# One held PSUM bank instead of two in a fast matrix product, GpSimd's sums cut in halves and rationed, and the last batch on attention's banks

## The chip, the cores and the metric

The kernel runs on one core of one Trainium2 chip. The metric is the device time of one execution in microseconds (us), median of several runs. All inputs lie in HBM when it starts, and all outputs must lie there when it ends. The engines of the core are TensorE (PE; its weight loads are listed apart as PEld), VectorE (DVE), ScalarE (ACT), GpSimd (POOL) and SyncE (SP, which here only issues transfers). Each runs its own list of instructions in order and waits for the others by semaphores.

## The reference

Two blocks one after the other, all in float32: attention that keeps the 32 largest scores of each row, then a Fourier mixing block with a two-layer MLP.

```python
# q, k, v: (8, 8, 576, 64): batch, heads, sequence, head dimension
scores = (1 / sqrt(64)) * matmul(q, k^T)
kth    = the 32nd largest score of each row
scores = where(scores >= kth, scores, -1e9)
attn   = softmax(scores)
a      = matmul(attn, v)
x      = a, heads side by side                      # (8, 576, 512)
mixed  = real(fft(fft(x, axis=1), axis=2))
u      = x + mixed
un     = (u - mean(u)) / sqrt(var(u) + 1e-6)        # over the 512 channels
out    = u + maximum(un @ w_ch1, 0) @ w_ch2         # w_ch1: 512x2048, w_ch2: 2048x512
```

## The kernel before

The program is written out by a Python loop over 288 steps of attention (32 pairs of heads, 9 tiles of 128 rows each) and a few more. In one step VectorE finds the 32 largest scores of one tile (four `max` of eight values and three `match_replace`), GpSimd turns two of those maxima into a shift and a bound (`nt`), ScalarE and GpSimd mask the scores, ScalarE takes the exponential (`expo`), and TensorE computes scores three tiles ahead, transposes the weights of two tiles back (`tpP`) and multiplies them with v (`o`). The work of the Fourier block and of the MLP of the batch before is put between these as "units" in a queue, so many in each step that it comes out even.

```python
    def bounds(i):                                   # end of step i, GpSimd
        Nt[i] = small.tile([P, 2], F32, name=f"nt_{i}", tag="nt", bufs=6)
        nc.gpsimd.tensor_tensor(out=Nt[i], in0=M8.pop(i)[:, 0:TOPK:TOPK - 1], in1=cc, op=ALU.mult)

    def mask(i):                                     # step i + 1
        w = Wk[i]
        nc.scalar.activation(out=w, in_=Ssb[i], func=AF.Relu, scale=-FAR, bias=Nt[i][:, 1:2])
        nc.gpsimd.tensor_tensor(out=w, in0=Ssb.pop(i), in1=w, op=ALU.subtract)
```

PSUM has eight banks. Attention holds five: two for scores (`ps_s`, tag "sp"), two for transposes (`ps_t`, tag "tp"), one for its output (`ps_o`). Everything else takes the three banks of `ps_m` in turn. A caller may hold one; the others then share what is left.

```python
    held, turn = set(), [0]

    def bank(shape, name, hold=False):
        while turn[0] in held:
            turn[0] = (turn[0] + 1) % 3
        n = turn[0]
        turn[0] = (n + 1) % 3
        t = ps_m.tile(shape, F32, name=name, tag=f"m{n}", bufs=1)
        if not hold:
            return t
        held.add(n)
        return t, lambda: held.discard(n)
```

Users of `bank` are the transform over tokens (`yp`, four a batch, each emptied by three ScalarE instructions), the transform over channels (`mp`, five a batch, emptied by ScalarE, or by VectorE in the first and last batch), the transposes before the MLP (`tpu`, five), the hidden layer (`hp`, 32), the second layer of the rest rows (`cp`) and the fast product below. The folds in front of the token transform (`sd`, `zw`, `fg`) run on GpSimd in batches 1 to 6; in the last batch half of them run on VectorE.

The second layer, hidden @ w_ch2, is done for batches 1 to 7 with seven products of half-size blocks in place of eight (`fast`, once for each of two chunks of 256 rows, 8 matmuls a product, two units a product). It needs four sums over the hidden layer (`mix`, GpSimd, 128x1024 each) and sums of the weights, which come in streamed. Two banks are held: X from `p1` to `p3`, Y from `p4` until VectorE has added the last two products.

```python
            def mix(dst, a, c, op=ALU.subtract):
                v = h()
                nc.gpsimd.tensor_tensor(out=v[dst], in0=v[a], in1=v[c], op=op)

            def summed(t, cols, src, n):                       # ScalarE empties, GpSimd adds
                ...                                            # (last batch: one VectorE instruction)
                nc.scalar.mul(out=room(n), in_=src, mul=rs[:, t:t + 1])
                nc.gpsimd.tensor_tensor(out=xt, in0=xt, in1=room(n), op=ALU.add)

            def p1(part):
                if part == 0:
                    got["X"], got["free X"] = bank([P, 2, DH], f"cx_{b}_{ch}", True)
                    mix("21", "21", "22", ALU.add)
                product(got["X"][:, 0, :], "11", b11, part, True)
                if part:
                    nc.scalar.copy(out=room(0), in_=got["X"][:, 0, :])
                    mix("11", "21", "11")
            def p4(part):    # Y, first half: "22" x T4; then summed(), mix("22", "22", "11")
            def p2(part):    # X, first half, on top of p1: "12" x B21; then summed(), mix("12", "12", "11")
            def p5(part):    # X, second half: "21" x T1; then summed()
            def p6(part):    # Y, first half: "11" x T2
            def p7(part):    # Y, second half: "22" x T3; then VectorE adds both halves to room(0), ...
            def p3(part):    # X, second half: "12" x B22; then summed(), X is freed, store
            # units in the order p1, p4, p2, p5, p6, p7, p3
```

At the end of a step come the lists of planned work; `pool0` (folds) runs before `bounds`, so a `mix` or a fold in front of it delays `nt` of that step. The sums of the weights are made once, every second step, four GpSimd instructions at a time:

```python
    for kc in range(NK):
        at(PER_BATCH + 14 + 2 * kc, "pool", lambda kc=kc: parts_of_w2(kc))
    ...
        run(i, "pool0")
        bounds(i)
```

Attention's output of a pair goes to token rows in `to_tokens` (`tpx`), which from the second batch on takes the bank of `ps_o`, one or more steps after `attend` has filled it (`o`); VectorE empties it at the end of the step. If the rows of x are not free yet, it waits in `pending`, and may then fall in a step in which `attend` fills the same bank again.

Of the kernel before, what the change touches and what calls it, by code (L numbers as in the profile page):

```python
# [9 lines left out]
F32 = mybir.dt.float32  # L10
# [54 lines left out]
def kernel(  # L65
# [544 lines left out]
    def dft_tokens(b, par, g2):  # L610
# [6 lines left out]
        y = y_of[b]  # L617
        yp = bank([P, 2, KQ], f"yp_{b}_{par}_{g2}")

# [38 lines left out]
    def dft_channels(b, t, quick=False):  # L658

        rows, y = ROWS[t], y_of[b]  # L660
        mp = bank([P, 2, DM // 2], f"mp_{b}_{t}")
        for par in range(2):
# [61 lines left out]
    def channels_first(b, t):  # L724

        rows = ROWS[t]
        ch, col = CHUNK_OF[t]
        if (b, ch) not in unT_of:
            unT_of[b, ch] = batp.tile(
                [P, NDT, CW[0]], F32, name=f"unT_{b}_{ch}", tag="fold_s" if ch == 0 else "y"  # L730
            )
        tp = bank([P, NDT, P], f"tpu_{b}_{t}")
        for dt in range(NDT):
            nc.tensor.transpose(
                tp[:, dt, 0:rows], x_of[b][0:rows, t, P * dt:P * (dt + 1)], ident[0:rows, 0:rows]
            )
        nc.scalar.copy(out=unT_of[b, ch][:, :, col:col + rows], in_=tp[:, :, 0:rows])  # L737
        return 0.6


# [14 lines left out]
    for _ in range(B - 1):  # L755
        for ch in range(2):
            stream += [(o, kc) for o in (T4, B21, T1, T2, T3) for kc in range(NK)]
            if ch == 0:
                stream += [(o, kc) for kc in range(NK) for o in (T1, B21)]
# [32 lines left out]

    def parts_of_w2(kc):

        t = batp.tile([P, 4, DH], F32, name=f"w2_t_{kc}", tag="fold_d")
        lo, hi = w2[:, kc, :], w2[:, NK + kc, :]
        for out_, in0, in1 in (
            (T1, lo[:, DH:], lo[:, 0:DH]), (T2, hi[:, DH:], t[:, T1]),
            (T3, hi[:, DH:], lo[:, DH:]), (T4, hi[:, 0:DH], t[:, T2]),
        ):  # L800
            nc.gpsimd.tensor_tensor(out=t[:, out_], in0=in0, in1=in1, op=ALU.subtract)
        at(now[0] + 1, "load2", lambda: nc.sync.dma_start(out=scr[:, 0:4, kc, :], in_=t))

    def mlp_units(b):
# [110 lines left out]
        def fast(ch):  # L917

            ta, tb = CHUNKS[ch][0], CHUNKS[ch][1]
            rs, got = rs_of[b], {}  # L920
            lo, hi = slice(0, DH), slice(DH, DM)
# [7 lines left out]

            def room(n):  # L930
                if ch == 0:
                    if not cts:
                        cts.append(batp.tile([P, 3, DM], F32, name=f"ct_{b}", tag="fold_s"))
                    return cts[0].rearrange("p t c -> p (t c)")[:, DH * n:DH * (n + 1)]
                o = NIT * CW[1] + DH * n
                return hTs[1].rearrange("p i c -> p (i c)")[:, o:o + DH]

            def product(dst, a, of, part, start=False):
                for kc in range(NK // 2 * part, NK // 2 * (part + 1)):
                    rhs, done = of(kc)  # L940
                    nc.tensor.matmul(  # L941
                        dst, lhsT=h()[a][:, kc, :], rhs=rhs, start=start and kc == 0,
                        stop=kc == NK - 1, skip_group_check=True,
                    )
                    done()

            def summed(t, cols, src, n):

                xt = x[:, t, cols]
                if last:  # L950
                    nc.vector.scalar_tensor_tensor(
                        out=xt, in0=src, scalar=rs[:, t:t + 1], in1=xt, op0=ALU.mult, op1=ALU.add
                    )
                    return
                nc.scalar.mul(out=room(n), in_=src, mul=rs[:, t:t + 1])
                nc.gpsimd.tensor_tensor(out=xt, in0=xt, in1=room(n), op=ALU.add)

            def mix(dst, a, c, op=ALU.subtract):
                v = h()
                nc.gpsimd.tensor_tensor(out=v[dst], in0=v[a], in1=v[c], op=op)  # L960

            def streamed(o):
                return lambda kc: take(o, kc)

            def store(t, steps):
                def go():
# [8 lines left out]
                else:  # L975
                    at(now[0] + steps, "load2", go)

            def p1(part):
                if part == 0:
                    got["X"], got["free X"] = bank([P, 2, DH], f"cx_{b}_{ch}", True)  # L980
                    mix("21", "21", "22", ALU.add)
                product(got["X"][:, 0, :], "11", b11, part, True)
                if part:
                    nc.scalar.copy(out=room(0), in_=got["X"][:, 0, :])
                    mix("11", "21", "11")

            def p4(part):
                if part == 0:
                    got["Y"], got["free Y"] = bank([P, 2, DH], f"cy_{b}_{ch}", True)
                product(got["Y"][:, 0, :], "22", streamed(T4), part, True)  # L990
                if part:
                    summed(tb, lo, got["Y"][:, 0, :], 2)
                    mix("22", "22", "11")

            def p2(part):
                product(got["X"][:, 0, :], "12", streamed(B21), part)
                if part:
                    summed(ta, lo, got["X"][:, 0, :], 3)
                    mix("12", "12", "11")

            def p5(part):
                product(got["X"][:, 1, :], "21", streamed(T1), part)
                if part:
                    summed(tb, hi, got["X"][:, 1, :], 2)

            def p6(part):

                product(got["Y"][:, 0, :], "11", streamed(T2), part, True)

            def p7(part):  # L1010
                product(got["Y"][:, 1, :], "22", streamed(T3), part)
                if not part:
                    return
                u2, u3, Y = room(0), room(1), got["Y"]

                def both():
                    nc.vector.tensor_tensor(out=u2, in0=Y[:, 0, :], in1=u2, op=ALU.add)
                    nc.vector.tensor_tensor(out=u3, in0=Y[:, 1, :], in1=u2, op=ALU.add)
                    got["free Y"]()

                def spread():
                    xa, xb = x[:, ta, hi], x[:, tb, :].rearrange("p (e c) -> p e c", e=2)
                    u3s = u3.rearrange("p (e c) -> p e c", e=1).to_broadcast([P, 2, DH])
                    if last:
                        for xt, u, t in ((xb[:, 0], u3, tb), (xb[:, 1], u3, tb), (xa, u2, ta)):
                            nc.vector.scalar_tensor_tensor(
                                out=xt, in0=u, scalar=rs[:, t:t + 1], in1=xt,
                                op0=ALU.mult, op1=ALU.add,
                            )
                    else:  # L1030
                        nc.scalar.mul(out=u3, in_=u3, mul=rs[:, tb:tb + 1])
                        nc.scalar.mul(out=u2, in_=u2, mul=rs[:, ta:ta + 1])
                        nc.gpsimd.tensor_tensor(out=xb, in0=xb, in1=u3s, op=ALU.add)
                        nc.gpsimd.tensor_tensor(out=xa, in0=xa, in1=u2, op=ALU.add)
                    store(tb, 1)

                if last:
                    both()
                    spread()
                else:  # L1040
                    def later():
                        both()
                        at(now[0] + 1, "act", spread)
                    late_next.append(later)

            def p3(part):
                product(got["X"][:, 1, :], "12", b22, part)
                if part:
                    summed(ta, hi, got["X"][:, 1, :], 3)
                    got["free X"]()  # L1050
                    store(ta, 3)

            def tails(half, part):
# [20 lines left out]
                (1.75, lambda f=f, part=part: f(part), "back")  # L1074
                for f in (p1, p4, p2, p5, p6, p7, p3) for part in range(2)
            ]
# [131 lines left out]
    for kc in range(NK):  # L1208
        at(PER_BATCH + 14 + 2 * kc, "pool", lambda kc=kc: parts_of_w2(kc))
    at(PER_BATCH + 14, "load2", lambda: nc.sync.dma_start(out=scr[:, B21], in_=w2[:, NK:, 0:DH]))  # L1210
# [102 lines left out]
    i, carry = 0, 0.0  # L1313
    while i < N + 4 or plan or queue:
        now[0] = i
# [21 lines left out]
        tok = []  # L1337
        if pending and pending[0][0] <= i:
            _, pp, pc = pending[0]
# [66 lines left out]
        for n in range(max(len(first), len(second))):  # L1406
            for ops in (first, second):
                if n < len(ops):
                    ops[n]()

        run(i, "pool0")
        bounds(i)
        if i < PER_BATCH:
# [46 lines left out]
```

## Time and profile before

| | before |
|---|---|
| device time, median of 3 runs | 1966.39 us (1964.42 to 1966.81) |
| profiled execution, span | 1964.0 us |
| PE busy | 1806.4 us (92%) |
| DVE busy | 1591.4 us (81%) |
| ACT busy | 1225.0 us (62%) |
| POOL busy | 961.6 us (49%) |

Attention and the MLPs of batches 0 to 6 fill the time up to about 1775 us. What is left is the transform and the MLP of the last batch. In a line of the costliest groups, the first word is the kernel's line, then the engine, the operation, what is written and read, shapes and count; after the bar come the busy time in us, the mean of one in ns, the idle time of the engine before them, and what ended it. A busy PE need not be one at its peak: matmuls are pipelined and their ends modelled. PEclk is the granted TensorE clock, 1.00 being full speed.

### The profile page before, as it was taken

The page shows a single profiled execution, that of the slowest core. Times are in us where ns is not written, and L with a number is a line of the kernel's source. Part 1 is how long each engine was busy: PE and PEld are TensorE (multiplying, and loading weights), DVE is VectorE, ACT ScalarE, POOL GpSimd, SP SyncE. Part 2 cuts the span into 40 slices and gives each one's busy share as a digit, 9 for nine tenths or more (in the row PEclk, how much of TensorE's full clock was granted, in tenths as well). Part 3 has the DMA queues.
Part 4 walks back from the last instruction along what each step waited for, and adds up shares of the span by engine and source line. Part 5 has one row for each costly group of instructions (what it writes and reads, how often), then busy time and mean ns, then how long its engine had stood idle before and what let it go on. Part 6 is the DMA issues. An engine that isn't in the chain of part 4 may idle for free.

```text
span 1964.0 us, 30502 instructions
## 1 busy us (share of the span) xinstructions
PE 1806.4 (92%) x9520; PEld 1275.7 (65%) x9520; DVE 1591.4 (81%) x3284; ACT 1225.0 (62%) x3128; POOL 961.6 (49%) x1196
## 2 busy tenths in 40 slices
PE   6666799998999999999999999999999999998899
PEld 3443465565667676776667776666667776676677
DVE  8999989998999979987888969897889878852110
ACT  6878657776767667665766757566666657651111
POOL 4767544636443663446525554436525464434111
PEclk8777899999999999999999999999999999999999
DMA  5323002210224130322204241242304241133151
GB/s 163 111 83 103 19 13 62 75 45 25 62 71 130 40 115 19 107 85 81 73 19 136 60 126 29 68 121 62 88 18 126 76 119 30 51 113 107 44 163 44
DMA packets 235633, 151.37 MB, mean 77 GB/s; under 512 B 135248, under 2 KB 226512, under 8 KB 235472
## 3 DMA queue, kind: packets, MB, share of 16 engines
q1 hardware_dynamic: 234688, 149.22, 26.4%
q8 instruction: 76, 1.25, 0.3%
q14 instruction: 85, 0.70, 0.1%
q10 hardware_dynamic: 784, 0.21, 0.0%
HBM read 134.65 MB, written 14.68 MB: 76 GB/s over the span
## 4 chain that ended last, share of the span: by engine, by line
PE 69%; POOL 15%; ACT 6%; issue 5%; DVE 5%; DMA 0%; SPq 0%; POOLq 0%; DVEq 0%; ACTq 0%
PE hp L820 23%; PE cx L941 7%; PE o L465 7%; PE cy L941 6%; PE sp L363 5%; PE tpP L428 5%; POOL wk L401 4%; PE yp L622 3%; PE cp L1064 3%; PE mp L670 3%; POOL hT L960 2%; PE cp L844 2%; DVE m L384 2%; POOL w L215 2%; POOL w L214 2%
## 5 line engine op out<-in xcount | busy, mean ns | idle before, releaser
L401 POOL TENSOR_TENSOR wk<-S,wk 128x576 f32<-128x576 f32 x288 | 408.2, 1417 | 753.4 <-ACT wk L400 725.3
L384 DVE MAX8 m<-wk 128x8 f32<-128x576 f32 x864 | 624.0, 751 | 5.2
L820 PE MATMUL hp<-unT,w 128*128 128x256 f32 (+1 forms) x2048 | 537.4, 409 | 3.7 <-ACT unT L737 2.1
L820 PEld LDWEIGHTS hp<-unT,w 128*128 128x128 f32 x2048 | 372.7, 190 | 127.9 <-issue 29.0
L386 DVE MATCH_REPLACE8 wk<-m,wk 128x576 f32<-128x576 f32 x576 | 427.9, 743 | 0.0
L400 ACT ACTIVATE wk<-S,nt 128x576 f32<-128x576 f32 x288 | 226.8, 788 | 94.4 <-POOL nt L393 93.4
L407 ACT ACTIVATE wk<-wk,nt 128x576 f32<-128x576 f32 x288 | 224.6, 780 | 75.6 <-POOL wk L401 74.2
L428 PE MATMUL tpP<-ident,wk 128*128 128x128 f32 x1152 | 187.6, 288 | 75.1 <-ACT wk L407 51.2
L428 PEld LDWEIGHTS tpP<-ident,wk 128*128 128x128 f32 x1152 | 143.0, 147 | 141.1 <-ACT wk L407 76.6
L384 DVE MAX8 m<-S 128x8 f32<-128x576 f32 x288 | 214.1, 743 | 15.8 <-ACT S L337 15.8
L431 ACT COPY PT<-tpP 128x512 f32<-128x512 f32 (+1 forms) x320 | 171.0, 546 | 74.0 <-PE tpP L428 71.2
L824 ACT ACTIVATE hT<-hp 128x320 f32<-128x320 f32 (+1 forms) x256 | 105.0, 410 | 179.8 <-PE hp L820 175.9
L386 DVE MATCH_REPLACE8 wk<-m,S 128x576 f32<-128x576 f32 x288 | 214.3, 744 | 0.0
L941 PE MATMUL cx<-w,hT 128*128 128x256 f32 x848 | 205.0, 388 | 10.0 <-issue 10.0
L465 PE MATMUL o<-PT,v 128*64 128x256 f32 (+3 forms) x1440 | 197.1, 418 | 9.1 <-DVE x L509 6.1
L941 PEld LDWEIGHTS cx<-w,hT 128*128 128x128 f32 x848 | 157.8, 194 | 39.7 <-issue 20.4
L960 POOL TENSOR_TENSOR hT<-hT 128x1024 f32<-128x1024 f32 x56 | 132.3, 2363 | 102.6 <-ACT hT L824 95.4
L363 PE MATMUL sp<-kT,qT 64*128 64x512 f32 (+1 forms) x528 | 165.9, 672 | 5.4 <-ACT means L1193 3.3
L366 ACT COPY S<-sp 128x512 f32<-128x512 f32 (+1 forms) x264 | 141.8, 588 | 44.8 <-PE sp L363 44.5
L465 PEld LDWEIGHTS o<-PT,v 128*64 128x64 f32 x1440 | 112.2, 154 | 79.4 <-issue 18.6
L941 PE MATMUL cy<-w,hT 128*128 128x256 f32 x648 | 156.2, 387 | 0.0
L941 PEld LDWEIGHTS cy<-w,hT 128*128 128x128 f32 x648 | 120.1, 193 | 24.6 <-issue 8.9
(166 smaller groups left out, 2164.0 us busy)
## 6 DMA issues: line engine op xcount, KB each, us to landing
w<-w_parts SPq DMA_DIRECT2D x624, 128.0 KB, 2.6
space<-in_moe_w_ch_dram SPq DMA_DIRECT2D x32, 512.0 KB, 3.6
nat<-in_q_dram SPq DMA_DIRECT2D x128, 64.0 KB, 2.2
v<-in_v_dram SPq DMA_DIRECT2D x128, 64.0 KB, 2.1
out_dram<-x SPq DMA_DIRECT2D x32, 256.0 KB, 2.1
nat<-in_k_dram SPq DMA_DIRECT2D x124, 64.0 KB, 2.2
w_s<-w_parts SPq DMA_DIRECT2D x48, 128.0 KB, 2.9
w_parts<-w_t SPq DMA_DIRECT2D x8, 512.0 KB, 3.0
```

The source lines that it names most:

```text
L363: nc.tensor.matmul(sp[r], lhsT=qT[hd, q_cols], rhs=kT[hd, :], start=True, stop=True)
L384: ops.append(lambda src=src, m8=m8: nc.vector.max(out=m8, in_=src))
L386: ops.append(lambda src=src, m8=m8: nc.vector.match_replace(w, m8, src, NEG))
L400: nc.scalar.activation(out=w, in_=Ssb[i], func=AF.Relu, scale=-FAR, bias=Nt[i][:, 1:2])
L401: nc.gpsimd.tensor_tensor(out=w, in0=Ssb.pop(i), in1=w, op=ALU.subtract)
L407: nc.scalar.activation(out=w, in_=w, func=AF.Exp, bias=Nt.pop(i)[:, 0:1], accum_out=den_t[pair % 3][:, c:c + 1],)
L428: nc.tensor.transpose(tp[:, c, :], p_sb[:, k0 + P * c:k0 + P * (c + 1)], ident)
L431: nc.scalar.copy(out=pt[:, NF * he:NF * (he + 1), col:col + w], in_=tp[:, :, o:o + w])
L465: nc.tensor.matmul(o[D * e:D * (e + 1), c0:c1], lhsT=vv[:, c, e, :], rhs=pt[:, 2 * NF if c == NF else NF * e + c, c0:c1], start=(c == 0), ...
L820: nc.tensor.matmul(hp[:, 0:w], lhsT=w1[:, dt, P * it:P * (it + 1)], rhs=unT[:, dt, 0:w], start=(dt == 0), stop=(dt == NDT - 1),)
L941: nc.tensor.matmul(dst, lhsT=h()[a][:, kc, :], rhs=rhs, start=start and kc == 0, stop=kc == NK - 1, skip_group_check=True,)
L960: nc.gpsimd.tensor_tensor(out=v[dst], in0=v[a], in1=v[c], op=op)
```

## The change

It has four parts.

1. The seven products are reordered to p2, p4, p1, p5, p6, p3, p7. Each of two banks, v (p2, p4) and w (the other five), is held alone, and the two halves of a bank hold successive products. p6 is added on top of p1, and p7 on top of that, so VectorE's two additions disappear. In the second chunk p2, p4 and p7 go to x by one VectorE instruction each instead of by ScalarE and GpSimd. It is for leaving two of the three banks to the others.
2. GpSimd's `mix` is cut in halves of 128x512, and these and its additions to x are put in a list (`sums`). Each step takes from it what a limit of 3.4 us, less its planned folds, allows; a product that needs a half forces it out (`need`). The sums of the weights are halved too, one half every step. It is for keeping long GpSimd work from in front of `nt` and the mask.
3. In the last batch, `yp` and `tpu` take attention's transpose banks and `mp` its score banks.
4. `to_tokens` doesn't run in a step in which `attend` fills the same bank (from the third batch on).

```diff
-        yp = bank([P, 2, KQ], f"yp_{b}_{par}_{g2}")
+        shape, name = [P, 2, KQ], f"yp_{b}_{par}_{g2}"
+
+        yp = ps_t.tile(shape, F32, name=name, tag="tp") if b == B - 1 else bank(shape, name)
...
-        mp = bank([P, 2, DM // 2], f"mp_{b}_{t}")
+        mp = ps_s.tile(shape, F32, name=name, tag="sp") if b == B - 1 else bank(shape, name)
...                                                    # tpu likewise, on ps_t
-            stream += [(o, kc) for o in (T4, B21, T1, T2, T3) for kc in range(NK)]
+            stream += [(o, kc) for o in (B21, T4, T1, T2, T3) for kc in range(NK)]
...
+    sums, summed = [], set()
+
+    def some_sums(limit):
+        while sums and sums[0][1] <= limit:
+            key, us, fn, _ = sums.pop(0)
+            limit -= us
+            fn()
+            summed.add(key)
+
+    def need(key):
+        while key not in summed:
+            got, _, fn, _ = sums.pop(0)
+            fn()
+            summed.add(got)
...
+            def mix(dst, a, c, op=ALU.subtract):
+                v = h()
+
+                def go(k0):
+                    k = slice(k0, k0 + NK // 2)
+                    nc.gpsimd.tensor_tensor(
+                        out=v[dst][:, k], in0=v[a][:, k], in1=v[c][:, k], op=op
+                    )
+                for n in range(2):
+                    later((dst, n), 1.25, lambda n=n: go(NK // 2 * n), True)
+
+            def to_x(t, cols, src, n):       # n None or last batch: one VectorE instruction,
+                ...                          # at the end of the next step (last batch: at once);
+                                             # else nc.scalar.mul to room(n), GpSimd's add by later()
...
+            def p2(part):
+                if part == 0:
+                    mix("21", "21", "22", ALU.add)
+                c = product("v", lo, "12", streamed(B21), part, True)
+                if part:
+                    to_x(ta, lo, c, None if ch else 0)
+
+            def p4(part):
+                c = product("v", hi, "22", streamed(T4), part, False)
+                if part:
+                    to_x(tb, lo, c, None if ch else 1)
+                    banks["v"][1]()
+
             def p1(part):
+                c = product("w", lo, "11", b11, part, True)
                 if part:
+                    to_x(ta, lo, c, 2)
                     mix("11", "21", "11")
+                    mix("12", "12", "11")
+                    mix("22", "22", "11")
+
+            def p5(part):
+                need((b, ch, ("21", part)))
+                c = product("w", hi, "21", streamed(T1), part, False)
                 if part:
+                    to_x(tb, hi, c, 3)
...                                          # p6: w lo, needs "11"; p3: w hi, needs "12"
+            def p7(part):
+                need((b, ch, ("22", part)))
+                c = product("w", lo, "22", streamed(T3), part, False)
                 if part:
+                    to_x(tb, slice(0, DM), c, None if ch else 2)
+                    store(tb)
+                    banks["w"][1]()
...
-                for f in (p1, p4, p2, p5, p6, p7, p3) for part in range(2)
+                for f in (p2, p4, p1, p5, p6, p3, p7) for part in range(2)
...
-        at(PER_BATCH + 14 + 2 * kc, "pool", lambda kc=kc: parts_of_w2(kc))
+        for half in range(2):
+            at(
+                PER_BATCH + 14 + 2 * kc + half, "pool",
+                lambda kc=kc, half=half: parts_of_w2(kc, half),
+            )
...
-        if pending and pending[0][0] <= i:
+
+        if pending and pending[0][0] <= i and (
+            i < 2 * PER_BATCH + 4 or (i - 3) % PER_PAIR not in (4, 8)
+        ):
...
+        planned = 1.5 * len(plan.get((i, "pool0"), [])) + 1.3 * len(plan.get((i, "pool2"), []))
         run(i, "pool0")
+        some_sums(max(3.4 - planned, 0.0))
         bounds(i)
```

## The prediction

> **What bounds the kernel now.** I read the page's busy shares first, then a table of stretches, then TensorE's waits in the steady part, then timelines where they are longest. In the table the columns are stretch, length, and busy time of PE, PEld, DVE, ACT and POOL, the granted clock, DMA share and rate.
>
> ```profile
> PE 1806.4 (92%) x9520; PEld 1275.7 (65%) x9520; DVE 1591.4 (81%) x3284; ACT 1225.0 (62%) x3128; POOL 961.6 (49%) x1196
> ...
> 780.00:900.00 120.00, 119.51 (x673) 86.21 (x671) 109.24 (x226) 81.14 (x211) 57.28 (x71) 1.00 0.30 85
> 905.00:1015.00 110.00, 99.21 (x528) 70.05 (x528) 89.16 (x190) 68.71 (x177) 57.66 (x75) 0.98 0.25 70
> ...
> 1775.00:1842.00 67.00, 53.84 (x268) 42.43 (x269) 21.34 (x32) 10.94 (x29) 25.49 (x35) 0.95 0.34 103
> ```
>
> Outside the transforms (780 to 900) PE is busy 99.6% of the time at full clock: nothing to win there. In a stretch where the next batch's transform meets the fast product of the batch before (905 to 1015) PE is idle 10.8 of 110 us and loses 2% of the clock. VectorE is at 81% there, so it doesn't forbid a gain. There are five such stretches (batches 2 to 6); the last batch's transform is 1775 to 1842. Of TensorE's waits from 655 to 1700 (total, times, longest) these are the first five:
>
> ```profile
> PE tpP L428 <- ACT wk L407: 9.6, 10, 2.5
> PE yp L622 <- ACT y L648: 8.6, 5, 4.6
> PE cx L941 <- issue: 8.2, 5, 3.2
> PE o L465 <- DVE x L509: 6.1, 3, 2.4
> PE mp L670 <- ACT us L687: 4.3, 3, 1.4
> ```
>
> With ten smaller ones the list sums to 45.9 us. The timeline of GpSimd at the second such stretch shows where the first and third come from:
>
> ```profile
> 906.46 4.80 POOL L960 TENSOR_TENSOR hT<-hT 128x1024 f32<-128x1024 f32 x2
> 911.22 2.37 POOL L597 TENSOR_TENSOR sd<-x 128x1024 f32<-128x1024 f32 x1
> 913.54 0.19 POOL L393 TENSOR_TENSOR nt<-m,cc 128x2 f32<-128x2 f32 x1
> 914.62 1.41 POOL L401 TENSOR_TENSOR wk<-S,wk 128x576 f32<-128x576 f32 x1 [0.89 <-ACT wk L400]
> 915.98 0.73 POOL L956 TENSOR_TENSOR x<-x,hT 128x256 f32<-128x256 f32 x1
> 916.67 2.38 POOL L960 TENSOR_TENSOR hT<-hT 128x1024 f32<-128x1024 f32 x1
> 919.00 2.51 POOL L566 TENSOR_TENSOR zw<-sd 128x512 f32<-128x512 f32 x2
> 921.46 0.20 POOL L393 TENSOR_TENSOR nt<-m,cc 128x2 f32<-128x2 f32 x1
> ```
>
> Two mixes and a fold stand in front of `nt`. From one `nt` to the next takes 7.9 us here and GpSimd is never free; ScalarE, in order, sits behind `nt`, with the copies that would free TensorE's banks behind it. TensorE shows it at 925.30: 3.21 us idle, and then 5.09 us for 16 matmuls which elsewhere take 3.6.
>
> **What the skill says.** "TensorE: Matmul & The Clock Gate", section "What's actually happening": after an idle window of some 3.4 us the array runs at half clock until it has been busy for such a window. The trace agrees: 5.09 against 3.6 us above, and mean clocks of 0.97 or 0.98 in the five stretches. "PSUM — Partial Sum Buffer", section "PSUM bank collisions raise a hardware error": access has to be guarded by bank, whichever columns are touched. The trace agrees in the tail, where p5 writes the other half of the bank that p2 has just filled and waits for VectorE to have read it:
>
> ```profile
> 1885.55 0.48 DVE L951 SCALAR_TENSOR_TENSOR x<-cx,gi,x 128x256 f32<-128x256 f32 x1 [2.90 <-PE cx L941]
> ...
> 1886.13 1.10 PE L941 MATMUL cx<-w_s,hT 128*128 128x256 f32 x4 [0.62 <-issue]
> ```
>
> "GPSIMD Engine Reference", section "3.1 Elementwise — side-by-side cycle accounting", puts two-input work at a constant number of cycles per element plus a dispatch. So a mix of 2363 ns (group of the mixes) should split into two of little over half; the trace's own 128x512 additions take 1280 ns, two make 2.56 us.
>
> **Part 1, the held banks.** Before, X and Y are held together while the folds' results arrive, and one bank is left for `yp`, `mp` and `tpu`: hence `yp` behind ScalarE's copy of the same bank (8.6 us) and `mp` (4.3), `tpu` (1.8, two smaller lines). After, one bank is held, and two consecutive tiles find two banks. I take 13 of 14.7 us.
>
> The price is in the rule of banks. Before, p1/p2 and p4/p6 alternate between X and Y, and only p5 follows directly on a read of its own bank. After, p4, p5, p6, p3 and p7 each write the bank whose other half has just been finished and must be emptied first. In the last batch's MLP nothing stands between the products: four more such gaps per chunk. One costs 0.62 us of idle plus the refilling of the pipe, about 0.8 us; 2 chunks x 4 x 0.8 = 6.4 us, and the last instruction on x is twice as wide as before (0.4 us more). In batches 1 to 6 the order of instructions puts attention's work between most products: mostly 0.4 to 1.3 us of matmuls, in a few places nothing. ScalarE needs 0.47 us for the emptying and a hand-over each way. There are (5 + 4) x 6 = 54 such places, less the 12 that p5 had before; at a guessed mean of 0.2 us the 42 lose about 8 us.
>
> **Part 2, GpSimd's sums.** I listed GpSimd's work between two `nt` in both programs and gave it the durations of the groups. For the stretch shown, the three heaviest steps go from about 8.7, 7.3 and 6.3 us to 5.3, 5.4 and 4.5, and what was pushed out fills the three after it (4.5, 5.4, 4.3). To each comes the 0.89 us in which it waits for ScalarE between `nt` and the mask. A tile of attention costs VectorE four MAX8 of 0.75, three MATCH_REPLACE8 of 0.744 and three loads of 0.083, 5.5 us; TensorE needs about 5.7. So 9.6 us becomes 6.2, near to what the others need, and most of the cause goes. I credit the `cx` wait (8.2) and those of the `tpP` waits that fall in the bursts (about 6 of 9.6): 14 us. GpSimd is still near its limit for five steps, and products now pull halves out late ("22" a step or less before p7): I charge 2 us per batch, 10 us. The weights' sums, every step instead of every second, flatten 2.9 us of GpSimd into 1.5; PE waits little there: 2 us.
>
> **Part 4.** The waits of `o` for VectorE's reading of `tpx` (6.1, and 1.6 in a smaller line) come from `to_tokens` and `attend` in one step: 7.7 us, gone.
>
> **The clock.** Lost clock in the five stretches, (1 - PEclk) x length, is 0.03x105 + 0.02x110 + 0.03x110 + 0.02x110 + 0.02x112 = 13 us. The long gaps go, so I credit 9.
>
> **Part 3, the last batch.** Between 1813 and 1834 PE waits 0.85, 0.78, 0.79 and 0.79 us for VectorE to empty the one free bank and 0.68, 0.68, 0.73 for ScalarE. With two banks each, VectorE's 1.6 us a tile (0.69 + 0.69 + 0.18) is under TensorE's 1.73 (eight matmuls), and only a `tpu` or two still waits: 5 us gained. The largest gap stays: 5.68 us at 1790 for the fold on VectorE, then half clock, because the order leaves the same number of products in front of it.
>
> **The sum.** Gains 13 + 14 + 7.7 + 9 + 2 + 5 = 51 us; charges 6.8 + 8 + 10 = 25 us. Net 26 us: about 1940. Since the 10 us charge may well be too large (the average load of the six steps, 5.8 us with the wait, fits), I put it at 1938 us, 1.4% faster.
>
> **Rivals.** (a) The bank becomes the new wait. ScalarE is in order, so an emptying can sit behind a copy or an exponential: at 1 us for each of the 42 places, 42 us would be lost in place of 8, and the change brings nothing (about 1972). For it: in the bursts ScalarE waits up to 4 us at a time. Against: these come from late `nt`, and ScalarE is only 62 to 65% busy. (b) Nearly all of the stretches' loss goes, because it is one knot: of 59 us of waits and clock in them 10 are left; with the other 7 us gained and the banks' 15 charged as above, 1925. For it: after the knot PE runs at 99.6%. Against: waits outside the knot remain (`tpP` for the exponential after the transforms, `tpq` for a copy). (c) VectorE becomes the bound. Its tiles of 5.5 us, plus norms and statistics, leave 12% to 19% in these stretches, 12 us even in the tightest (655 to 760, 92.7 of 105 busy): it caps batch 2, not the sum. (d) Later additions to x hold back the stores and so `to_tokens` two batches on: it has more than a batch of slack, so I expect nothing.
>
> **Range and chances.** The gains are measured waits; what is uncertain is how many come back as others. 1916 to 1958 holds 8 of 10. The 2% limit is at 1927, inside rival (b): faster 0.28, within 2% 0.66, slower 0.06.
>
> **What would show it.** `yp` behind `y` under 2 us in all, `o` behind `x` gone, intervals between two `nt` in the stretches under 7 us, PEclk 0.99 or more there: parts 1, 2 and 4 right. Four to five gaps of 0.6 us per chunk in the tail instead of one: the bank's price. `mp` back to back after 1810: part 3. I am wrong if `cw` is among PE's longest waits in the stretches with more than 15 us, or if these still keep over 5 us of idle PE each.

## The result and the profile after

| | before | after |
|---|---|---|
| device time, median | 1966.33 us | 1974.11 us (1973.28 to 1975.30) |
| ratio to before, 95% interval | | 1.0042 (1.0024 to 1.0059) |

The kernel became 0.4% slower; 1938 us was predicted. The page's busy line of the kernel after, and the groups of the hidden layer and of the bank w (the last field is the idle time of the engine just before them and what ended most of it):

```profile
PE 1803.6 (91%) x9520; PEld 1271.9 (65%) x9520; DVE 1588.8 (81%) x3274; ACT 1220.0 (62%) x3108; POOL 961.9 (49%) x1246
...
L848 PE MATMUL hp<-unT,w 128*128 128x256 f32 (+1 forms) x2048 | 544.9, 413 | 13.7 <-DVE x L992 11.6
...
L1036 PE MATMUL cw<-w,hT 128*128 128x256 f32 x1056 | 256.6, 389 | 26.8 <-POOL hT L980 14.6
```

TensorE's work is the same, it only waits elsewhere: `hp`, whose rows come from ScalarE, now waits 11.6 us for line 992, VectorE's addition of a product to x. The table of stretches of the kernel after (columns as in the prediction):

```profile
905.00:1015.00 110.00, 103.38 (x541) 72.89 (x540) 91.14 (x193) 70.64 (x180) 56.75 (x78) 0.97 0.24 67
1130.00:1240.00 110.00, 99.25 (x523) 71.11 (x523) 86.52 (x184) 67.30 (x171) 53.42 (x74) 0.94 0.24 66
1355.00:1465.00 110.00, 97.67 (x510) 70.59 (x509) 84.32 (x178) 65.75 (x168) 54.48 (x75) 0.94 0.25 69
1580.00:1692.00 112.00, 107.05 (x590) 77.09 (x589) 92.95 (x197) 73.60 (x188) 58.70 (x81) 1.00 0.23 66
1775.00:1842.00 67.00, 60.51 (x309) 49.71 (x308) 20.73 (x33) 12.01 (x33) 26.27 (x38) 0.95 0.32 97
```

In the kernel before the second and third of these stretches were:

```profile
1130.00:1240.00 110.00, 102.16 (x541) 72.01 (x540) 91.49 (x194) 71.49 (x185) 55.19 (x74) 0.97 0.25 70
1355.00:1465.00 110.00, 99.96 (x528) 70.62 (x526) 89.25 (x190) 69.06 (x178) 57.71 (x75) 0.98 0.25 69
```

The first and fourth are better than before (PE was busy 99.21 and 104.95 us), the second and third are worse, by 2.9 and 2.3 us, and have a granted clock of only 0.94. TensorE's waits from 655 to 1700 of the kernel after (total, times, longest):

```profile
PE cw L1036 <- POOL hT L980: 14.0, 10, 2.2
PE hp L848 <- DVE x L992: 11.6, 2, 8.2
PE tpu L738 <- DVE x L992: 9.2, 2, 7.4
PE cw L1036 <- issue: 3.6, 8, 1.0
PE tpP L428 <- ACT wk L407: 3.4, 3, 2.0
```

The waits of before that the prediction credited (`yp` for y 8.6, `cx` 8.2, `o` for x 6.1, `mp` 4.3) are gone, `cx` but for the 3.6 us of `cw` for "issue", and `tpP` fell from 9.6 to 3.4. In their place stand four long waits for line 992 (20.8 us) and ten for GpSimd's halves (14.0 us). TensorE's timeline at the second of the four:

```profile
1187.71 1.89 PE L1036 MATMUL cw<-w,hT 128*128 128x256 f32 x8
1189.53 0.46 PE L738 MATMUL tpu<-ident,x 64*128 64x64 f32 x4
1197.43 1.09 PE L738 MATMUL tpu<-ident,x 128*128 128x128 f32 x4 [7.44 <-DVE x L992]
1198.31 1.06 PE L428 MATMUL tpP<-ident,wk 128*128 128x128 f32 x4
```

and VectorE's in the same stretch:

```profile
1196.54 0.74 DVE L992 SCALAR_TENSOR_TENSOR x<-cw,gi,x 128x512 f32<-128x512 f32 x1
```

The first line is the last half of `p7` (the trace counts two instructions for each float32 matmul, so the eight of a product are x16): the bank w is full at 1189.5. The next `tpu` finds a free bank, the one after it gets w because w is next in turn, but VectorE starts to empty w only at 1196.54, at the end of the next step, after a whole tile's search for the 32 largest. The two other banks had been emptied by 1190.4, by ScalarE's copies of the two `tpu` before. TensorE stands 7.4 us, and the transposes that follow take 1.06 and 1.09 us in place of 0.60: the granted clock is 0.50 from 1194 to 1202.

Setting the ends of the 288 masks of the two kernels side by side, step by step, gives the balance: in five bursts, each at the beginning of one of the five stretches (steps 114 to 120, 150 to 156, 186 to 192, 222 to 228, 258 to 264) the kernel after gains 5.8, 6.4, 3.8, 6.7 and 6.3 us, 29 us together. Around the waits for w it loses 6.5 (steps 162 to 168), 11.9 (192 to 204) and 8.8 us (234 to 240), and 4.2 us more in steps 48 to 66, where the weights' sums are made. The other steps together lose another 6.5 us, so that the kernel after is 8.9 us late at the last mask. The gain was there, and most of what ate it is a new wait.

### The profile page after: what moved, and what is told of

Read it like the earlier page. It is cut to its first block, busy times and chain, and to the rows that moved or that the text cites. A ratio compares the mean times of both kernels' runs of the same rounds, so it can differ in the third digit from the quotient of the medians.

```text
span 1971.8 us, 30544 instructions
## 1 busy us (share of the span) xinstructions
PE 1803.6 (91%) x9520; PEld 1271.9 (65%) x9520; DVE 1588.8 (81%) x3274; ACT 1220.0 (62%) x3108; POOL 961.9 (49%) x1246
## 4 chain that ended last, share of the span: by engine, by line
PE 69%; POOL 12%; DVE 8%; issue 5%; ACT 4%; DMA 0%; SPq 0%; POOLq 0%; DVEq 0%; ACTq 0%
PE hp L848 24%; PE cw L1036 10%; PE o L465 6%; PE sp L363 5%; PE tpP L428 5%; POOL wk L401 4%; PE cv L1036 4%; DVE m L384 3%; PE yp L624 3%; DVE wk L386 3%; PE cp L1105 3%; POOL w L215 2%; POOL w L214 2%; PE cp L872 2%; PE sp_t L333 1%
## 5 line engine op out<-in xcount | busy, mean ns | idle before, releaser
L848 PE MATMUL hp<-unT,w 128*128 128x256 f32 (+1 forms) x2048 | 544.9, 413 | 13.7 <-DVE x L992 11.6
L848 PEld LDWEIGHTS hp<-unT,w 128*128 128x128 f32 x2048 | 376.8, 192 | 140.4 <-issue 34.3
L1036 PE MATMUL cw<-w,hT 128*128 128x256 f32 x1056 | 256.6, 389 | 26.8 <-POOL hT L980 14.6
L1036 PEld LDWEIGHTS cw<-w,hT 128*128 128x128 f32 x1056 | 193.7, 192 | 72.8 <-issue 25.4
L980 POOL TENSOR_TENSOR hT<-hT 128x512 f32<-128x512 f32 x112 | 140.7, 1272 | 124.8 <-ACT hT L852 95.7
L363 PE MATMUL sp<-kT,qT 64*128 64x512 f32 (+1 forms) x528 | 159.0, 662 | 4.2 <-ACT means L1234 3.3
L1036 PE MATMUL cv<-w,hT 128*128 128x256 f32 x432 | 102.7, 382 | 1.2 <-DVE x L992 1.2
L1036 PEld LDWEIGHTS cv<-w,hT 128*128 128x128 f32 x432 | 78.4, 190 | 16.2 <-issue 4.3
```

The costliest lines, as they stand in the source:

```text
L363: nc.tensor.matmul(sp[r], lhsT=qT[hd, q_cols], rhs=kT[hd, :], start=True, stop=True)
L848: nc.tensor.matmul(hp[:, 0:w], lhsT=w1[:, dt, P * it:P * (it + 1)], rhs=unT[:, dt, 0:w], start=(dt == 0), stop=(dt == NDT - 1),)
L1036: nc.tensor.matmul(dst, lhsT=h()[a][:, kc, :], rhs=rhs, start=start and kc == 0, stop=kc == NK - 1, skip_group_check=True,)
```

## The experiments

All times are medians; the ratio is to runs of the kernel before on the same chip, with its 95% interval. The medians of before lie between 1965.57 and 1967.03 us on these chips, so a difference of one or two us between rows may be the chip's.

| run | edit | us | ratio |
|---|---|---|---|
| e1 | after, w given back late | 1946.71 | 0.9899 (0.9883 to 0.9916) |
| e2 | after, p7 emptied by ScalarE | 1949.01 | 0.9906 (0.9892 to 0.9921) |
| e3 | after, weights' sums whole | 1972.29 | 1.0027 (1.0016 to 1.0038) |
| e4 | before + part 4 | 1963.29 | 0.9982 (0.9975 to 0.9989) |
| e5 | before + part 3 | 1958.96 | 0.9959 (0.9944 to 0.9974) |
| e6 | e1, limit 6.0 | 1973.13 | 1.0028 (1.0011 to 1.0044) |
| e7 | e1, a bank for each half in the tail | 1938.18 | 0.9854 (0.9839 to 0.9868) |
| e8 | e1, no list | 2014.56 | 1.0245 (1.0222 to 1.0267) |
| e9 | e7, limit 4.0 | 1933.65 | 0.9838 (0.9823 to 0.9853) |
| e10 | e7, weights' sums whole | 1933.82 | 0.9841 (0.9827 to 0.9856) |
| e11 | e7, sums' transfer one step earlier | 1934.53 | 0.9844 (0.9828 to 0.9861) |
| e12 | e7, limit 4.0, weights' sums whole | 1931.84 | 0.9827 (0.9811 to 0.9843) |

**e1: the bank is given back where VectorE's late addition is issued.** The kernel before did this for Y (`got["free Y"]()` stood inside the late `both`); the change gives w back in `p7` itself.

```diff
 def to_x(t, cols, src, n, then=lambda: None):
-                        late_next.append(add)
+                        late_next.append(lambda: (add(), then()))
 ...                                   # the other ways to x call then() at once
 def p7(part):
-                    to_x(tb, slice(0, DM), c, None if ch else 2)
+                    to_x(tb, slice(0, DM), c, None if ch else 2, banks["w"][1])
-                    banks["w"][1]()
                                        # v in p4 likewise
```

> The changed kernel, but a bank is given back only when VectorE's late addition that empties it has been written out. Theory (bank handed on while still full): the waits of hp and tpu for x (11.6 and 9.2 us between 655 and 1700) go to under 2 us, the clock in the five stretches comes back to 0.98 or more, and the time falls by 20 to 34 us from 1974 to about 1940 to 1954. Rival (GpSimd's rationed sums, forced out late, are what holds TensorE): these waits only turn into others and the time stays above 1965. Second rival (one bank less for a step costs as much as it frees): yp and mp show waits of 10 us or more again, as before the change.

Measured 1946.71 us, 27.4 less than the kernel after. TensorE's waits from 655 to 1700 in e1; none for line 992 is left:

```profile
PE cw L1038 <- POOL hT L980: 14.0, 10, 2.2
PE cw L1038 <- issue: 3.9, 10, 1.0
PE tpP L428 <- ACT wk L407: 3.4, 3, 1.9
```

The two bad stretches in e1:

```profile
1130.00:1240.00 110.00, 106.51 (x562) 75.15 (x561) 97.38 (x206) 74.71 (x191) 53.01 (x76) 0.98 0.21 57
1355.00:1465.00 110.00, 103.92 (x547) 73.40 (x545) 93.06 (x199) 73.13 (x188) 50.46 (x74) 0.98 0.19 51
```

PE goes from 99.25 and 97.67 us to 106.51 and 103.92, and the clock from 0.94 to 0.98. Against the 27.4 us stand 20.8 us of waits and the slowed work after them. The ends of the masks show that nothing else changed: e1 gains 5.2 us on the kernel after in steps 162 to 168, 9.4 in 192 to 204 and 12.2 in 234 to 246, the places of the waits, and within 2 us nothing anywhere else.

**e2: the other way to the same end.** ScalarE empties w at once in the second chunk too, and GpSimd adds.

```diff
-                    to_x(tb, slice(0, DM), c, None if ch else 2)
+                    to_x(tb, slice(0, DM), c, 2)
```

> The changed kernel, but p7 of the second chunk is emptied by ScalarE at once (and added by GpSimd) instead of by VectorE at the end of the next step; the bank is given back as before. Theory (it is the lateness of VectorE's reading, not the number of banks): same gain as the late release, 1940 to 1954, and no wait of hp or tpu for x. Rival (rationed sums): over 1965, and more wait of cw for GpSimd than 14 us, as GpSimd gets six more additions of 1.28 us.

Measured 1949.01 us, and again no wait for line 992. Two different cures of the late emptying give nearly the same time, so the cause is the time between `p7` and its emptying. It isn't VectorE's load, which e1 leaves as it was, nor the number of banks, which e2 leaves as it was.

**e3: the weights' sums whole, every second step, as before.**

```diff
-        for half in range(2):
-            at(PER_BATCH + 14 + 2 * kc + half, "pool", lambda ...: parts_of_w2(kc, half))
+        at(PER_BATCH + 14 + 2 * kc, "pool", lambda ...: [parts_of_w2(kc, half) for half in range(2)])
```

> The changed kernel, but the sums of the weights are made as before, four at a time every second step. Theory (the halves meet the transfer of the part before in the one buffer, and GpSimd waits 6.2 us for it): the time falls by 3 to 5 us to about 1970, and the wait of GpSimd for that transfer falls from over 6 us to about 3. Rival (the start's drift explains the 5 us): no difference.

Measured 1972.29 us, 1.8 less: the sign as expected, the size less than expected, and the two intervals of the ratio overlap. GpSimd's wait for the transfer fell from 15.3 us (longest 6.2) to 3.5. In the profiled executions e3 gains 4.2 us on the kernel after in steps 48 to 66, where the sums are made, and has given all of it back by step 264. e10 and e11 take it up.

**e4: part 4 alone, on the kernel before.**

> The kernel before with part 4 alone: no to_tokens in a step of attend. Prediction: the waits of o for x (7.7 us) go, and with them one or two spans of half clock: 6 to 10 us faster, about 1958. Rival (attention's tokens only come later and the gap moves): within 3 us of 1966.

Measured 1963.29 us beside 1967.03 of before: 3.7 us. The wait of `o` for x (6.1 us) is gone from the waits, but that of `cx` rose from 8.2 to 9.9.

**e5: part 3 alone, on the kernel before.** The diff is that of part 3.

> The kernel before with part 3 only (the last batch's yp and tpu on the transpose banks, mp on the score banks). If the prediction's term holds, the waits of 0.7 to 0.85 us between mp and tpu after 1810 us go and the time falls by 5 us: 1960 to 1963. Rival: the one free bank only hid VectorE's own pace, so the waits move to other tiles and the time stays within 2 us of before (1964 to 1968). The fold's gap of some 5 us near 1790 stays in both.

Measured 1958.96 us beside 1966.15: 7.2 us, against 5 predicted. TensorE's waits from 1775 us to the end in e5, the whole list:

```profile
PE yp L624 <- DVE fg L550: 5.6, 1, 5.6
PE cx L945 <- issue: 1.9, 3, 0.6
PE tpu L738 <- ACT unT L741: 0.2, 1, 0.2
```

In the kernel before, `mp` and `tpu` waited 6.3 us in this list. The fold's 5.6 us stays, as predicted. Up to the last mask e5 and before are within 0.1 us of each other, so the gain lies in the last batch alone.

**e6: a larger limit of the list, on e1.**

```diff
-        some_sums(max(3.4 - planned, 0.0))
+        some_sums(max(6.0 - planned, 0.0))
```

> The changed kernel with the bank given back only after VectorE has emptied it (1946.7 us), and the limit of the list at 6.0 in place of 3.4 us a step. If the list is rationed too tightly, TensorE's waits of cw for GpSimd's halves (14.0 us, 10 times) fall under 6 us and the time is 1938 to 1943. Rival: with longer GpSimd steps nt and the mask come late again, waits of tpP for the exponential's tile and cx-like bursts return, and the time is the same or longer (1946 to 1960).

Measured 1973.13 us, 26.4 more than e1: the rival's direction held, and its range was too small. The waits of `cw` for GpSimd did fall, from 14.0 to 4.6. GpSimd's timeline in e6 shows the price:

```profile
1154.06 0.20 POOL L393 TENSOR_TENSOR nt<-m,cc 128x2 f32<-128x2 f32 x1
1155.14 1.41 POOL L401 TENSOR_TENSOR wk<-S,wk 128x576 f32<-128x576 f32 x1 [0.89 <-ACT wk L400]
...
1156.67 1.42 POOL L550 TENSOR_TENSOR fg<-zw 128x254 f32<-128x254 f32 x2
1158.04 3.72 POOL L980 TENSOR_TENSOR hT<-hT 128x512 f32<-128x512 f32 x3
1161.72 0.72 POOL L1008 TENSOR_TENSOR x<-x,hT 128x256 f32<-128x256 f32 x1
1162.40 0.19 POOL L393 TENSOR_TENSOR nt<-m,cc 128x2 f32<-128x2 f32 x1
```

ScalarE's, in the same stretch of e6:

```profile
1162.63 0.77 ACT L400 ACTIVATE wk<-S,nt 128x576 f32<-128x576 f32 x1 [4.60 <-POOL nt L393]
1163.31 0.46 ACT L1004 ACTIVATE hT<-cw,gi 128x256 f32<-128x256 f32 x1
```

and TensorE's:

```profile
1163.86 2.47 PE L1038 MATMUL cw<-w,hT 128*128 128x256 f32 x5 [5.59 <-issue]
```

Three halves (line 980) and an addition to x (line 1008) stand, with folds (line 550), before `nt`, which comes 8.3 us after the one before it. ScalarE waits for `nt`, and its emptying of the shared bank (`hT<-cw`, 0.46 us of work) stands behind that in its order; TensorE waits for the emptying. The page calls this wait "issue"; the releaser is seen only by laying the three timelines side by side.

**e7: in the last batch each half has a bank of its own, on e1.**

```diff
 def half_bank(name, cols):
+    if last and cols == hi:            # second halves: a tile of ps_s, one for each of v and w
+        ...
+        return banks[name, "hi"][:, hi]
 # p4 and p5: start=last in place of start=False
```

> As the late give-back (1946.7 us), and in the last batch each product half has a bank of its own (the second halves on the score banks, which attention no longer uses). If the prediction's price of the shared bank in the tail is right (0.8 us a place, four or five places a chunk), the gaps of 0.6 to 0.8 us behind VectorE in the last MLP go and the time falls by 5 to 7 us: 1940 to 1942. Rival: the gaps are VectorE's own pace or a refilling of the pipe at each new product; then they stay, 1945 to 1948.

Measured 1938.18 us, 8.5 less than e1, more than the 5 to 7 expected. The kernel after shows it on TensorE like this:

```profile
1883.47 3.62 PE L1036 MATMUL cw<-w,hT 128*128 128x256 f32 x16
1887.71 1.97 PE L1036 MATMUL cw<-w,hT 128*128 128x256 f32 x8 [0.62 <-issue]
```

From 1883.47 to 1887.71 are 4.24 us for 16 matmuls. e7, where `p1` is followed by `p5` in another bank:

```profile
1855.95 3.62 PE L1044 MATMUL cw<-w,hT 128*128 128x256 f32 x16
1859.40 1.89 PE L1044 MATMUL cwh<-w,hT 128*128 128x256 f32 x8
```

3.45 us for the same, so 0.79 us a place. e7 takes away all ten places, five in each chunk, which makes 7.9 of the 8.5 us. The prediction had counted the eight that are new, and put 6.4 us on them; at 0.79 us they are 6.3. Its 0.4 us for the wider last instruction is not tested, as e7 keeps that instruction.

**e8: no list, on e1.** Every half and every addition is issued where its product ends.

```diff
 def later(key, us, fn, soon=False):
-                if last:
-                    need((b, ch, key))
+                need((b, ch, key))
```

> As the late give-back (1946.7 us), but nothing is kept in the list: every half of a mix and every addition to x is issued to GpSimd where its product ends, as before the change (the weights' sums stay halved). If GpSimd's long steps were half of the knot, as the prediction credits (14 us gained, 10 charged), the bursts return in part and the time is 1950 to 1965, with tpP and cw waits in the stretches of 905 to 1015 and the like. Rival: freeing the bank alone undid the knot and the list only costs: the waits of cw for GpSimd go, and the time is 1933 to 1943.

Measured 2014.56 us, 67.9 more than e1, beyond both theories. GpSimd's timeline in e8:

```profile
1405.13 7.42 POOL L979 TENSOR_TENSOR hT<-hT 128x512 f32<-128x512 f32 x6
```

and TensorE's:

```profile
1417.88 2.47 PE L1037 MATMUL cw<-w,hT 128*128 128x256 f32 x5 [9.17 <-issue]
```

In the new order three mixes, six halves, fall due at once at the end of `p1`. Without the list they are one block of 7.4 us in front of `nt`. In the old order they came one product at a time. So part 1's order needs the list to be bearable. What the list would bring with the old order no run shows.

**e9: a limit of 4.0, on e7.** The diff is that of e6 with 4.0.

> Late give-back and banks of their own in the tail (1938.2 us), and the list's limit at 4.0 in place of 3.4 us: a step with one planned fold takes two halves in place of one (2.5 us left of 4.0), one without still takes no more than three. If the waits of cw for GpSimd (14.0 us, 10 times, five of them 2.4 us) come from halves that the folds pushed out until the product forced three at once, most of them go and the time is 1928 to 1934. Rival, which the limit of 6.0 showed in the large: each half more in a step delays nt by 1.25 us and ScalarE's emptying of the bank behind it; then the time is 1938 to 1950.

Measured 1933.65 us, 4.5 less than e7. TensorE's waits from 655 to 1700 in e9:

```profile
PE cw L1044 <- issue: 9.8, 11, 2.7
PE cw L1044 <- ACT hT L1004: 5.6, 4, 3.7
PE tpP L428 <- ACT wk L407: 4.8, 5, 1.9
PE cw L1044 <- POOL hT L980: 2.2, 2, 1.1
```

(The five long waits for halves in e7 are 2.2 us each, not 2.4 as the expectation has it.) The forced halves cost 2.2 in place of 14.0 us, but 11 us come back as late emptyings and late exponentials. So both sides of the expectation are in it, and the waits as a sum fall by only 1 us. The rest may be the clock, an estimate, as PEclk has two digits: in three of the five stretches PEclk is 1.00 where e7 has 0.98, in the first (655 to 760) 0.98 where e7 has 1.00, which is 0.02 x (332 - 105) = 4.5 us. Of the three limits tried, 3.4, 4.0 and 6.0, the middle one is best: the list must clear the halves before a product needs them, and three of them with folds in front of one `nt` were too many in e6.

**e10 and e11: the weights' sums, on e7.** e10 has the edit of e3. e11 keeps the halves and issues their transfer in the same step:

```diff
-            at(now[0] + 1, "load2", lambda: nc.sync.dma_start(out=scr[:, 0:4, kc, :], in_=t))
+            at(now[0], "load2", lambda: nc.sync.dma_start(out=scr[:, 0:4, kc, :], in_=t))
```

> Late give-back and banks of their own in the tail (1938.2 us), and the weights' sums whole, every second step, as before the change. In the changed kernel alone this brought 1.9 us; the theory is that it is independent of the banks, so 1935 to 1937 here. Rival: in the changed kernel it was within the scatter; then 1937.5 to 1939.5.

> Late give-back and banks of their own in the tail (1938.2 us), and the transfer of the weights' sums issued in the step of the second half, not one step later. The sums' one buffer is then free a step earlier, so GpSimd's wait of 6.2 us for that transfer near 352 us and TensorE's gap of 2.7 us behind it should go: 1934 to 1937. Rival: the transfer waits in the queue behind the loads of the next batch anyway, or holds them up while it waits for GpSimd; then 1937.5 to 1941.

Measured 1933.82 us (4.4 less than e7) and 1934.53 us (3.7 less). GpSimd's wait for its own transfer, from 300 to 420 us, in e7:

```profile
POOL w_t L811 <- DMA w_parts<-w_t: 15.5, 5, 6.2
```

in e10:

```profile
POOL w_t L811 <- DMA w_parts<-w_t: 2.9, 1, 2.9
```

and in e11:

```profile
POOL w_t L811 <- DMA w_parts<-w_t: 7.0, 4, 3.2
```

The sums have one buffer. Halving them put the transfer a step later, and the next half in front of the next `nt` waited for it. Either cure takes most of that away, and in the profiled executions each gains 4.2 us on e7 in steps 48 to 66, just what the change had lost there. So the buffer was the cause, and not the number of GpSimd's instructions, which e11 leaves as it was.

**e12: e9 and e10 together.**

> Late give-back, banks of their own in the tail, limit 4.0 and the weights' sums whole, together. The limit brought 4.5 us and the whole sums 4.4 us on the same base of 1938.2 us, in different stretches (after 600 us and from 300 to 420 us). If they add up, 1928.5 to 1931. Rival: both remove the same delay, carried on through the running budget of the steps; then 1932 to 1935.

Measured 1931.84 us, on the boundary of the rival: of 4.5 + 4.4 us 6.3 are realised. The profiled executions suggest why. From step 48 on, before which neither edit acts, e9 gains 3.4 us on e7 up to the last mask, e10 2.9 and e12 6.5, so there the two do add up. But e9 and e10 were 1.3 and 2.5 us ahead of e7 by step 48 already, by luck of the start, where e12 was level with it. It is the fastest version: 1.7% under before, 42 us under the change as it was made.

## Why the prediction was wrong

**The step that failed: part 1, the held banks.** It said that with one bank held "two consecutive tiles find two banks", took 13 of 14.7 us, and looked for the price only inside a bank, between its halves. It did not follow when a bank is given back and when it is emptied. The change gives w back in `p7`, and in the second chunk VectorE empties it up to a step later. That cost 27.4 us (e1), more than the whole predicted net of 26. Rival (d) had the late additions in view, but asked only what they do to the stores. The sign of rival (a), the bank as the new wait, was right, its mechanism not: the emptying was late on VectorE's list, not ScalarE's, and it is luck that its 1972 us lies near the 1974 measured.

**The net of parts 1 and 2 before the tail** was about right once w is cured: 13 + 14 us and 9 of clock, less 10 and 8, make 18. In the profiled executions e1 gains 22.7 us on the kernel before from step 66 to the last mask; 4 to 7 of them are part 4's (below), which leaves 16 to 19, an estimate. The single terms were less good. The intervals between two `nt` in the first such stretch of the kernel after:

```profile
909.76 0.21 POOL L393 TENSOR_TENSOR nt<-m,cc 128x2 f32<-128x2 f32 x1
...
915.90 0.20 POOL L393 TENSOR_TENSOR nt<-m,cc 128x2 f32<-128x2 f32 x1
...
921.13 0.18 POOL L393 TENSOR_TENSOR nt<-m,cc 128x2 f32<-128x2 f32 x1
...
939.91 0.20 POOL L393 TENSOR_TENSOR nt<-m,cc 128x2 f32<-128x2 f32 x1
...
948.40 0.19 POOL L393 TENSOR_TENSOR nt<-m,cc 128x2 f32<-128x2 f32 x1
```

The first two are 6.1 and 5.2 us, as worked out, where before showed 7.9; the last is 8.5 us, in which GpSimd itself waits 6.2 us for ScalarE. The charge of 10 us for late halves was of the right kind and too small: 14.0 us of waits, and slow clock after most of the long ones (last section). So the clock's credit of 9 us was too large: in e1 PEclk is 0.98 in four of the five stretches, 0.02 x 442 = 8.8 us lost where before lost 13. The split between parts 1 and 2 stays open: part 2 was counted as a gain of its own, but no run has it without part 1's order; e8 shows only what that order costs without the list.

**Part 4** was over-sized: 7.7 us credited, 3.7 measured (e4). 1.7 us of the wait came back as `cx`. In the profiled executions e4 gains 6.8 us on before from step 48 to the last mask, and gives back 4.8 behind it, with the same waits: from 1820 to 1840 us its granted clock is 0.74, before's 1.00. So a part of the gain went with the clock; that execution (1965.43 us) is the slowest of e4's twenty.

**The weights' sums** had the wrong sign: a gain of 2 us predicted, a loss of 1.8 (e3) to 4.4 us (e10). Flattening GpSimd's work was counted; the single buffer behind it, with its transfer one step later, was not.

**Part 3** held, at 7.2 us in place of 5, and **the shared bank in the tail** held, at 6.3 us for the eight new places in place of 6.4 (e7). **Attention's share of that price** (8 us) isn't separated by any run: in e1 the waits that could belong to it, `cw` for issue and for ScalarE, are 5.9 us in all.

**The sum of the misses.** 27.4 (w) + 4 (part 4) + 4 to 6 (weights' sums) is 35 to 37 us, and 1974 - 1938 is 36. The sum leaves out part 3's 2 us more. The terms come from separate runs, and e12 shows that such terms need not add up, so the agreement is no proof that nothing else is in it.

**The signs named in advance.** `yp` behind y, `o` behind x, `mp` after 1810 us and the tail's gaps came out as written. The `nt` intervals did not all fall under 7 us: the longest in the five stretches are 8.4 to 14.5 us in the kernel after and 8.2 to 10.3 in e1 (9.6 to 13.5 before). Nor was PEclk 0.99 or more in all five. The sign of being wrong, over 5 us of idle PE in a stretch, came in four of the five (7.5, 6.6, 10.8 and 12.3 us), and the two largest led to line 992; `cw` waits 14.0 us for GpSimd, and 19.6 with its two other lines.

## What to carry to other kernels

When a buffer is handed on, compare two places in the program: where the order gives it back, and where its last reader is issued. If that reader sits on a list for a later step, the next user of that buffer inherits the whole delay, even where others are free. A list that rations one engine's work has two costs, forced work when it is too slow and late small results when it is too fast, so it needs a sweep rather than an argument; and where work is cut finer, check the buffer and the transfer behind it.

## What the runs showed of the hardware

The same idle time did not always have the same price. In e1 TensorE stands 2.23 or 2.24 us for a forced half once in each of the five stretches, always behind the same kinds of instructions (`cw`, `tpP`); three of these places:

```profile
717.35 1.99 PE L1038 MATMUL cw<-w,hT 128*128 128x256 f32 x8 [2.23 <-POOL hT L980]
...
1152.47 2.64 PE L1038 MATMUL cw<-w,hT 128*128 128x256 f32 x8 [2.23 <-POOL hT L980]
...
1593.29 3.13 PE L1038 MATMUL cw<-w,hT 128*128 128x256 f32 x8 [2.24 <-POOL hT L980]
```

The eight instructions take 1.99, 2.64 and 3.13 us; in the two other places, at 931.03 and 1371.11, 3.06 and 2.82 us. The granted clock (third figure from the right) after the first two gaps shown:

```profile
718.00:721.00 3.00, 3.00 (x23) 2.85 (x22) 1.52 (x3) 0.98 (x3) 2.23 (x4) 1.00 0.45 132
1154.00:1157.00 3.00, 3.00 (x12) 2.67 (x11) 1.12 (x3) 1.86 (x6) 2.04 (x4) 0.50 0.03 5
```

In four of the five places it falls to 0.50 for 3.4 us, and only 0.7 to 1.2 us after TensorE has resumed (worked out from stretches of half a us); in the first it stays at 1.00. So the half clock can follow a gap of 2.2 us, shorter than the idle window of some 3.4 us that the Trainium skill gives ("TensorE: Matmul & The Clock Gate", section "What's actually happening"), but need not; what decides wasn't tried. The time that it lasts agrees with the busy window given there. (The prediction's own example, a gap of 3.21 us, is shorter than the idle window too.) Such a gap thus costs 2.2 us of waiting and, where the clock falls, an estimated 0.5 x 3.4 = 1.7 us more.

Cutting a `mix` into halves was nearly free: the group of the halves has a mean of 1272 ns, two make 2.54 us, where one whole took 2.36, so 0.18 us for the extra instruction.
